# Three expert blocks of 512 tokens in place of six of 256, and one ring of four tiles for the first-layer results

## The chip, the core and the metric

The kernel runs on one core of one Trainium2 chip. The metric is the device time of one execution in microseconds (us), as the median of several runs. The engines are named as in the profile: PE is TensorE's matmul, PEld its weight load, DVE is VectorE, ACT ScalarE, POOL GpSimd, SP SyncE. A queue (SPq, POOLq) is where an engine issues transfers.

## The reference

An attention over 8 sequences of 576 tokens with 8 heads of 64 makes 4608 rows of 512 numbers; four heads see the last 32 positions, four see every 32nd. Its result goes through a mixture of 8 experts, of which each token uses one:

```python
logits = x @ w_gate + modality_bias[modality_id]
e_idx = np.argmax(logits, axis=1)
...
gate_w = probs[np.arange(N), e_idx]
for e in range(E):
    mask = e_idx == e
    h = np.maximum(x[mask] @ w1[e], 0.0)
    out[mask] = gate_w[mask, None] * (h @ w2[e])
```

`x` is 4608 x 512, `w1[e]` 512 x 1024, `w2[e]` 1024 x 512, all float32. With the inputs that the reference draws, three experts get all tokens. After the second pair of sequences they hold 731, 1115 and 458 tokens, after the third 1093, 1693 and 670, and at the end 1435, 2291 and 882 (worked out from the reference itself).

## The kernel before, in words

**Attention and routing.** 32 units (16 of local heads, 16 of strided) go through PE in an order written out by hand (L1250 to L1280). After each pair of sequences `finish_pair` turns rows and columns, and `route` computes the expert of each token, its place in the expert's region of a DRAM buffer `xd`, and nine scatters of 128 token rows each, which POOL issues (L687 to L699). The rows of a token are 528 words: 512 numbers, the token's number and its gate weight.

**Blocks.** The second half of the program is a row of expert blocks. A slot is 256 tokens of one expert (`SLOT`). `PHASES` says after which pair of sequences how many slots are drawn up: 2 after the second pair, 4 after the third, 20 places after the last. `slots` (L732) computes on DVE, with small instructions on tables of 8 experts, which expert and which rows each slot has; the first six slots are blocks of one slot each, the last phase has five blocks of two slots of one expert (`NDOUBLE`), two of one slot (`NSINGLE`), and one half slot of 128 tokens (`half_ffn`). Slots beyond those would run in a conditional part (`rest`, L1325), which is not taken here. The list of blocks is `plan` (L1190): six single blocks (names 0_0, 0_1, 1_0 to 1_3), five double ones, two single ones.

**One block, `ffn` (L1046).** Eight steps f, one for each 128 columns of the first layer. Step f brings the weights of f (1024 columns: 512 of each layer) into a high and a low part: ACT copies and rounds (`wh`, L1098), DVE subtracts (`wl`, L1101), two pieces of 512 each. `up` (L1050) is 12 matmuls into one PSUM bank, three products for each of the 4 pieces of 128: `wh`·`xh`, `wh`·`xl`, `wl`·`xh`; the stationary side is the weight, the moving side the tokens, so each streams 256 columns in a single block and 512 in a double one. ACT then makes `hh` (L1064), DVE the low part `hl` (L1065). `down` (L1068) is three matmuls of 512 columns for each 128 tokens: 6 in a single block, 12 in a double one. `down` of step f runs two steps later (`LAG`). In the last `down` ACT scales the sums by the gate weight (`y`, L1081) and POOL scatters them to the output (L1082).

**Buffers.** `hh` and `hl` of a single block come from two pools of four tiles; a double block takes four tiles `h2` in places that the attention used (`xc2`, `xc3`). `xh` and `xl` of single blocks have two buffers each of 256 columns, those of double blocks two of 512 (`xta`, `xtb`).

**Tokens of a block.** `gather` (L1211) has SP load the rows of a slot from `xd` (`fx`, L870), once all scatters up to that phase's pair of sequences have landed. `send` (L1218) copies the rows as 16-bit halves on DVE (`rows`, L1012, two instructions) and has SP transpose them, SBUF to SBUF (`cols`, L1018, two DMAs). `split` (L1222) copies them back on DVE (`xs`, L1029), ACT rounds the high part (`xh`, L1043), DVE subtracts the low part (`xl`, L1044). The first block takes another way: PE transposes its tokens (`turn_tokens`, L988, 8 transposes) and ACT and DVE split them. `between` (L1290) says at which step of block k what is done: gather of block k+3 in step 7, send of block k+2 in step 6 (its second slot in step 7), split of block k+1 in step 4 (second slot in step 5). It also takes up pieces of the routing of the last pair (`pop`).

**What sets the order.** In the attention PE's order is the one of the program; from the first block on a scheduler decides it when the program is built, on all engines. Each engine then works in that order. Blocks 0 and 1 still have PE work of the last pair's routing between their matmuls: 36 transposes of 128 x 128 (`xl`, `xs`), the gating matmuls (`lg`), three more transposes (`lt`) and a few small ones.

## Time and profile before

| | us |
|---|---|
| median of 3 runs | 574.73 (574.72 to 575.61) |
| the profiled execution | 579.18 |
| its span, first to last instruction | 577.1 |
| PE busy in it | 548.6 (95%) |
| DVE / ACT / POOL busy | 377.5 / 312.2 / 91.0 |
| DMA | 137.00 MB, mean 237 GB/s |

The profiled execution has its own time, 4.45 us over the median; 2.1 us of it lie outside the span. Durations below are of this execution. A row of the timeline has the start in us from the span's start, the length, engine, line, operation, what is written and read, shape and count; in square brackets stands how long the engine stood still before it and what ended that. Rows of equal instructions that overlap are merged. A matmul's length includes its way through the array, so the distance of two starts, not the length, is what a matmul costs.

### The profile page before, as it was taken

The page shows a single profiled execution, that of the slowest core. Times are in us where ns is not written, and L with a number is a line of the kernel's source. Part 1 is how long each engine was busy: PE and PEld are TensorE (multiplying, and loading weights), DVE is VectorE, ACT ScalarE, POOL GpSimd, SP SyncE. Part 2 cuts the span into 40 slices and gives each one's busy share as a digit, 9 for nine tenths or more (in the row PEclk, how much of TensorE's full clock was granted, in tenths as well). Part 3 has the DMA queues.
Part 4 walks back from the last instruction along what each step waited for, and adds up shares of the span by engine and source line. Part 5 has one row for each costly group of instructions (what it writes and reads, how often), then busy time and mean ns, then how long its engine had stood idle before and what let it go on. Part 6 is the DMA issues. An engine that isn't in the chain of part 4 may idle for free.

```text
span 577.1 us, 13498 instructions
## 1 busy us (share of the span) xinstructions
PE 548.6 (95%) x5273; PEld 462.5 (80%) x5273; DVE 377.5 (65%) x940; ACT 312.2 (54%) x651; POOL 91.0 (16%) x108
## 2 busy tenths in 40 slices
PE   7889789798999999999999999999999999999995
PEld 4777667676888999899988888888888888889984
DVE  7967867869967897787965735635734734547541
ACT  3657676658876566576653344344353443456642
POOL 2020230320612611011010020020020011021320
PEclk9979999999999999999999999999999999999998
DMA  7979888888989999999896582482482553455621
GB/s 262 349 232 316 290 279 285 291 316 276 411 220 344 408 318 411 286 332 277 270 258 259 154 268 78 136 284 92 118 249 109 148 179 114 126 199 176 247 92 39
DMA packets 65942, 137.00 MB, mean 237 GB/s; under 512 B 40383, under 2 KB 40767, under 8 KB 58816
## 3 DMA queue, kind: packets, MB, share of 16 engines
q1 hardware_dynamic: 59168, 112.46, 60.7%
q0 software_dynamic: 6416, 23.37, 11.0%
q8 instruction: 43, 0.70, 0.5%
q10 hardware_dynamic: 288, 0.24, 0.2%
q14 instruction: 27, 0.22, 0.1%
HBM read 107.97 MB, written 24.30 MB: 229 GB/s over the span
## 4 chain that ended last, share of the span: by engine, by line
PE 85%; DVE 5%; issue 4%; ACT 2%; DMA 2%; SPq 1%; POOL 0%; POOLq 0%; DVEq 0%; ACTq 0%
PE h L1056 35%; PE o L1074 35%; PE s L398 2%; PE o L446 2%; PE oa L544 2%; DMA lqk<-in_qkl 2%; PE xs L236 2%; PE ss L492 2%; PE lg L621 2%; PE xl L236 1%; PE t L236 1%; ACT xc L557 1%; PE ts L236 1%; DVE eb L530 1%; DVE mx L411 1%
## 5 line engine op out<-in xcount | busy, mean ns | idle before, releaser
L1056 PE MATMUL h<-xh,wh 128*128 128x256 f32 (+1 forms) x408 | 132.9, 326 | 0.2 <-ACT wh L1098 0.2
L1056 PE MATMUL h<-xh,wl 128*128 128x256 f32 (+1 forms) x408 | 132.8, 326 | 0.0
L1056 PE MATMUL h<-xl,wh 128*128 128x256 f32 (+1 forms) x408 | 132.6, 326 | 0.0
L1074 PE MATMUL o<-wh,h 128*128 128x512 f32 x320 | 105.8, 392 | 0.0
L1101 DVE TENSOR_TENSOR wl<-lqk,wh 128x512 fp32r<-128x512 f32 x104 | 68.0, 688 | 52.7 <-ACT wh L1098 46.6
L1098 ACT CAST wh<-raw 128x512 fp32r<-128x512 f32 x102 | 58.5, 622 | 58.7 <-PE o L1074 54.9
L1082 POOL DMA_INDIRECT out<-y,le x36 | 39.4, 1093 | 320.9 <-ACT y L1081 313.9
L1101 DVE TENSOR_TENSOR wl<-raw,wh 128x512 fp32r<-128x512 f32 x102 | 66.5, 689 | 32.5 <-ACT wh L1098 31.9
L1098 ACT CAST wh<-lqk 128x512 fp32r<-128x512 f32 x104 | 60.0, 620 | 49.7 <-PE o L1074 45.9
L1056 PEld LDWEIGHTS h<-xh,wh 128*128 128x128 f32 x408 | 77.3, 189 | 9.7 <-ACT wh L1098 0.4
L1056 PEld LDWEIGHTS h<-xl,wh 128*128 128x128 f32 x408 | 77.3, 189 | 8.9
L1056 PEld LDWEIGHTS h<-xh,wl 128*128 128x128 f32 x408 | 77.3, 189 | 7.7 <-DVE wl L1101 0.4
L1074 PEld LDWEIGHTS o<-wh,h 128*128 128x128 f32 x320 | 60.1, 188 | 13.7
L1074 PE MATMUL o<-wl,h 128*128 128x512 f32 x160 | 62.9, 393 | 0.0
L1065 DVE SCALAR_TENSOR_TENSOR h<-h,h 128x512 fp32r<-128x512 f32 x40 | 27.7, 692 | 48.9 <-ACT h L1064 48.9
L1064 ACT ACTIVATE h<-h 128x512 fp32r<-128x512 f32 x40 | 23.9, 599 | 50.3 <-PE h L1056 50.3
L1074 PE MATMUL o<-wh,hh 128*128 128x512 f32 x128 | 51.1, 399 | 0.0
L1074 PE MATMUL o<-wl,hh 128*128 128x512 f32 x128 | 50.5, 395 | 0.0
L1074 PE MATMUL o<-wh,hl 128*128 128x512 f32 x128 | 49.3, 393 | 0.0
L1064 ACT ACTIVATE hh<-h 128x256 fp32r<-128x256 f32 x64 | 24.6, 385 | 24.8 <-PE h L1056 22.7
L1074 PEld LDWEIGHTS o<-wl,h 128*128 128x128 f32 x160 | 30.0, 188 | 6.7
L689 POOL DMA_INDIRECT xd<-xa,posi x20 | 21.7, 1087 | 77.4 <-DVE eb L530 28.9
(211 smaller groups left out, 849.4 us busy)
## 6 DMA issues: line engine op xcount, KB each, us to landing
lqk<-in_w SPq DMA_DIRECT2D x26, 1024.0 KB
raw<-in_w SPq DMA_DIRECT2D x24, 1024.0 KB
lqk<-in_qkl SPq DMA_DIRECT2D x32, 296.0 KB
vv<-in_vl SPq DMA_DIRECT2D x32, 292.5 KB
sqk<-in_qks SPq DMA_DIRECT2D x32, 288.0 KB
fx<-xd SPq DMA_DIRECT2D x16, 528.0 KB
vs<-in_vs SPq DMA_DIRECT2D x16, 320.0 KB
xd<-in_nul SPq DMA_DIRECT2D x9, 528.0 KB
```

The source lines that it names most:

```text
L236: nc.tensor.transpose(dst, src, ident)
L398: nc.tensor.matmul(sp[32 * u:32 * u + 32, 128 * m:128 * m + 128], q[:, i, :], kd[:, :, i:i + 2, :], start=False, stop=True, skip_group_che ...
L446: nc.tensor.matmul(o[64 * jj:64 * jj + 64, k, :], et[:, 2 * (k // 2) + bb, 2 * (k % 2) + jj, :, :].rearrange("p g q -> p (g q)"), vv[:, 4 ...
L492: nc.tensor.matmul(s[32 * u:32 * u + 18, 36 * i:36 * i + 36], qk[:, 32 + r, :], qk[:, r:r + 65:64, :], start=False, stop=True, skip_group_ ...
L689: ins = nc.gpsimd.indirect_dma_start(xd[:], IOA(ap=posi[:, i:i + 1], axis=0), x[:, j, :], None)
L1056: nc.tensor.matmul(hp, wx[:, a1], x[:, c, :], start=(k == 0), stop=(k == 11))
L1064: evicted[f] = nc.scalar.activation(hh[:], hp, AF.Relu)
L1065: nc.vector.scalar_tensor_tensor(hl[:], hp, 0.0, hh.bitcast(F32), ALU.max, ALU.subtract)
L1074: nc.tensor.matmul(os[h], hx[:, m], w[:, 512:1024], start=(f == 0 and i == 0), stop=(f == 7 and i == 2))
L1082: outs.add(nc.gpsimd.indirect_dma_start(out, IOA(ap=le[:, 0:1], axis=0), y[:], None, bounds_check=NT - 1, oob_is_err=False))
L1098: ins = nc.scalar.copy(wh[:, c], raw[:, c])
L1101: nc.vector.tensor_tensor(wl[:, c], raw[:, c], wh[:, c].bitcast(F32), ALU.subtract)
```

## The change

`PHASES` now has 30 places in the last phase, and the first two phases are drawn up in pairs of slots: `slots` halves the number of full slots of each expert (`prs`) and gives out pairs. `plan` becomes three double blocks (0, 1_0, 1_1), then the five double, two single and the half block as before. The first block's 512 tokens are all turned by PE (`turn_first(0)`, `turn_first(1)`), its first `up` is made in two halves of 256 columns, and its step f now takes up routing pieces twice. All blocks share a ring of four tiles for `hh`/`hl`: two lie where the first weights `ws0`, `ws1` of the first block lay, two are new. `xh`/`xl` of 256 columns with two buffers become one of 512, used by block 0 and by the first of the two late single blocks. `cols` has one buffer. The table `PLACES` moves the token work: in a double block the next block's first slot is sent in step 2 and split in step 4, the second sent in step 4 and split in step 6, and the block after that gathered in step 5; in a single block the send is in step 1, the split and the gather in step 5.

```diff
-PHASES = ((1, 2), (2, 4), (3, 20))
+PHASES = ((1, 2), (2, 4), (3, 30))
-POPF = (2, 2)
+POPF = 2
-FIRST, SECOND, SPLIT, SEND, GATHER, FAR = 1, 3, 4, 6, 7, 6
-CPAD = 1216
+FIRST, SECOND = 1, 2
+PLACES = {2: (2, 4, 4, 6, 5), 1: (1, 5, 0, 0, 5)}
+CPAD = 1048
...
+        prs = smalls([P, E], I32, f"prs{ph}")
+        nc.vector.tensor_copy(prs[:], nblk[:])
+        nc.vector.tensor_single_scalar(prs[:], prs[:], 1, ALU.arith_shift_right)
+        sums(0, prs)
+        nc.vector.scalar_tensor_tensor(off[:, 0, :], exc[:, 0, :], -2.0, used[ph][:], ALU.mult, ALU.add)
...
+    def h_tile(f):
+        return ring[f % 4]
...
     def split_first(f):
-        w = ap.tile([P, 2, 512], F32R, tag=f"xc{2 + f}", bufs=2, name=f"ws{f}")
+        w = ap.tile([P, 2, 2 * SLOT], F32R, tag=f"xc{2 + f}", bufs=2, name=f"ws{f}")
+        ring.append(w)
...
+    def turned_pair(n):
+        return [pre.tile([P, 4, 2 * SLOT], F32R, tag=t, bufs=1, name=f"{t}{n}") for t in ("xh", "xl")]
...
-        if far:
-            cols = ap.tile([P, 2, 2, 4, P], U16, tag=f"xc{n[-1]}", bufs=1, name=f"cols{n}")
-        else:
-            cols = fp.tile([P, 2, 2, 4, P], U16, tag="cols", bufs=1, name=f"cols{n}")
+        cols = fp.tile([P, 2, 2, 4, P], U16, tag="cols", bufs=1, name=f"cols{n}")
...
         def up(f, wh, wl):
             hp = pa(f"h{n}{f}")[:, 0:w]
-            k = 0
-            for c in range(4):
-                a1 = slice(P * c, P * c + P)
-                for wx, x in ((wh, xh), (wh, xl), (wl, xh)):
-                    nc.tensor.matmul(hp, wx[:, a1], x[:, c, :], start=(k == 0), stop=(k == 11))
-                    k += 1
...
+            for q in (slice(0, SLOT), slice(SLOT, w)) if first and f == 0 else (slice(0, w),):
+                k = 0
+                for c in range(4):
+                    a1 = slice(P * c, P * c + P)
+                    for wx, x in ((wh, xh), (wh, xl), (wl, xh)):
+                        nc.tensor.matmul(hp[:, q], wx[:, a1], x[:, c, q], start=(k == 0), stop=(k == 11),
+                                         skip_group_check=first)
+                        k += 1
+            hh, hl = (h_tile(f + 2)[:, i, 0:w] for i in range(2))
...
-            slots_of = [(i,) for i in range(n)]
+            slots_of = [(2 * i, 2 * i + 1) for i in range(n // 2)]
...
         if n == nu + 1:
             while calm and next(calm[0], calm) is not calm:
                 pass
-            turn(0, split_first)
+            turn_first(0)
+    turn_first(1)
     scatter_rows(len(todo))
...
             if k == 0 and f == SECOND:
                 while 1 not in tables:
                     pop(1)
-                gather(2)
-            if f == SPLIT:
-                if k + 1 == len(plan):
-                    turn(k + 1)
-                split(k + 1, 0)
-            if f == SPLIT - 1 + parts(k + 1):
-                split(k + 1, 1)
-            if f == SEND:
-                send(k + 2, 0)
-            if f == GATHER:
-                gather(k + 3, 0)
-                send(k + 2, 1)
-                gather(k + 3, 1)
-            pop(POPF[k > 0])
+                load(1, 0)
+                gather(1, 0)
+                gather(1, 1)
...
+            for part in range(2):
+                if part < parts(k + 1):
+                    if f == sends[part]:
+                        send(k + 1, part)
+                    if f == splits[part]:
+                        split(k + 1, part)
+            if f == PLACES[parts(k)][4]:
+                gather(k + 2, 0)
+                gather(k + 2, 1)
+            pop(POPF)
```

Three places show how the built order moves. The names carry the block and the step: `h0_01` is block 0, step 1 after the change, `h0_01` before is block 0_0, step 1; the last number of a name is a counter. First PE at the start of the first block; `xt` are the tokens turned by PE, `oa` and `ob` the last unit of the attention. Before:

```order
L236 MATMUL xt0_00_3043<-cf_sb_65,fx0_00_2882 128x128 x4
L236 MATMUL xt0_01_3053<-cf_sb_65,fx0_00_2882 128x128 x4
L544 MATMUL oa15_3066<-eb15_3006,vs15_2880 64x126 x8
L551 MATMUL ob15_3075<-ec15_3007,vs15_2880 64x72 x2
L1056 MATMUL h0_00_3103<-xh0_0_3041,ws0_3050 128x256
```

With the change:

```order
L237 MATMUL xt000_3046<-cf_sb_65,fx00_2885 128x128 x4
L237 MATMUL xt001_3056<-cf_sb_65,fx00_2885 128x128 x4
L545 MATMUL oa15_3069<-eb15_3009,vs15_2883 64x126 x8
L552 MATMUL ob15_3078<-ec15_3010,vs15_2883 64x72 x2
L237 MATMUL xt010_3084<-cf_sb_65,fx01_2943 128x128 x4
L237 MATMUL xt011_3091<-cf_sb_65,fx01_2943 128x128 x4
L1057 MATMUL h0_00_3124<-xh0_3044,ws0_3053 128x256
```

Eight transposes stand ahead of the first matmul of the experts.

Second, ACT from the first token copy on (`xc33` is the attention's last result, `xc30` the routing's). Before:

```order
L984 CAST ws1_3060<-raw0_2836 128x512
L557 COPY xc33_143<-oa15_3066 128x28x18
L558 COPY xc33_143<-ob15_3075 128x4x18
L1098 CAST wh0_00_3095<-raw0_2836 128x512
L1098 CAST wh0_01_3099<-raw0_2836 128x512
L579 COPY xc30_140<-xl300_3195 128x512
L1064 ACTIVATE hh0_00_3116<-h0_00_3103 128x256
```

With the change:

```order
L985 CAST ws1_3063<-raw0_2839 128x512
L558 COPY xc33_143<-oa15_3069 128x28x18
L559 COPY xc33_143<-ob15_3078 128x4x18
L1095 CAST wh0_00_3116<-raw0_2839 128x512
L1095 CAST wh0_01_3120<-raw0_2839 128x512
L1003 CAST xh0_3044<-xt010_3084 128x2x256
L1003 CAST xh0_3044<-xt011_3091 128x2x256
L580 COPY xc30_140<-xl300_3215 128x512
```

The high part of the second 256 tokens stands behind two weight copies.

Third, DVE where the tokens of the first phase-1 slots are handled; `rows1_01` is the second slot of the next block, `wl0_06` the weights of step 6. Before, that slot's block is two blocks away:

```order
L1065 SCALAR_TENSOR_TENSOR hl0_06_3420<-h0_06_3406,hh0_06_3419 128x256
L1012 COPY rows1_00_3423<-fx1_00_3265 128x2x512 x2
L889 COPY le1_00_3429<-fx1_00_3265 128x8
L651 TENSOR_TENSOR lo3_3444<-lo3_3444,bias_68 128x8
L1101 TENSOR_TENSOR wl0_11_3537<-raw0_2836,wh0_11_3536 128x512 x2
```

With the change:

```order
L1062 SCALAR_TENSOR_TENSOR h0_3114<-h0_04_3423,h0_3114 128x512
L1030 COPY xs1_00_3438<-cols1_00_3268 128x1024 x2
L1098 TENSOR_TENSOR wl0_06_3471<-lqk1_84,wh0_06_3470 128x512 x2
L1044 TENSOR_TENSOR xl1_00_3442<-xs1_00_3438,xh1_00_3441 128x2x256
L685 TENSOR_TENSOR po3_3503<-rk3_3506,ohb3_3403 128x72
L1044 TENSOR_TENSOR xl1_00_3442<-xs1_00_3438,xh1_00_3441 128x2x256
L1016 COPY rows1_01_3447<-fx1_01_3260 128x2x512 x2
L887 COPY le1_01_3453<-fx1_01_3260 128x8
L1062 SCALAR_TENSOR_TENSOR h1_3115<-h0_05_3477,h1_3115 128x512
```

The copy back of the first slot (`xs1_00`), which waits for its transposes, now stands ahead of the weights of step 6 of the same block.

## Rows read from the trace of the kernel before

**Rows 1.** The page: tenths of PE busy and of its granted clock, 40 slices.

```profile
PE   7889789798999999999999999999999999999995
PEclk9979999999999999999999999999999999999998
```

**Rows 2.** Windows: stretch, length, busy PE PEld DVE ACT POOL, PE clock, DMA share, GB/s.

```profile
147.22:175.10 27.88, 27.71 (x216) 24.03 (x213) 21.52 (x60) 20.34 (x45) 11.40 (x9) 1.00 0.95 312
175.10:198.06 22.96, 22.96 (x150) 20.48 (x148) 20.43 (x53) 14.02 (x28) 11.28 (x11) 1.00 1.06 366
198.06:289.62 91.56, 91.56 (x584) 83.11 (x582) 74.88 (x177) 58.06 (x116) 10.07 (x9) 1.00 1.02 320
289.62:506.64 217.02, 217.02 (x944) 176.77 (x942) 114.40 (x186) 90.24 (x156) 19.21 (x18) 1.00 0.55 170
```

**Rows 3.** Timeline of PE: first matmul of successive steps in a single and two double blocks.

```profile
237.54 0.28 PE L1056 MATMUL h<-xh,wh 128*128 128x256 f32 x1
...
240.36 0.28 PE L1056 MATMUL h<-xh,wh 128*128 128x256 f32 x1
...
346.25 0.39 PE L1056 MATMUL h<-xh,wh 128*128 128x512 f32 x1
...
351.81 0.39 PE L1056 MATMUL h<-xh,wh 128*128 128x512 f32 x1
...
390.57 0.40 PE L1056 MATMUL h<-xh,wh 128*128 128x512 f32 x1
...
396.08 0.40 PE L1056 MATMUL h<-xh,wh 128*128 128x512 f32 x1
```

**Rows 4.** Timeline of PE: two neighbouring matmuls of 256 columns, and two of 512.

```profile
238.01 0.28 PE L1056 MATMUL h<-xl,wh 128*128 128x256 f32 x1
238.13 0.28 PE L1056 MATMUL h<-xh,wl 128*128 128x256 f32 x1
...
395.85 0.39 PE L1074 MATMUL o<-wh,h 128*128 128x512 f32 x1
```

**Rows 5.** Timeline of PE around the first matmul of the experts, and transposes further on.

```profile
145.06 1.09 PE L236 MATMUL xt<-cf_sb,fx 128*128 128x128 f32 x8
146.08 1.08 PE L544 MATMUL oa<-eb,vs 126*64 126x126 f32 x16
147.22 0.39 PE L1056 MATMUL h<-xh,ws 128*128 128x256 f32 x1
...
155.94 0.60 PE L236 MATMUL xl<-cf_sb,xa 128*128 128x128 f32 x4
156.37 0.60 PE L236 MATMUL xl<-cf_sb,xb 128*128 128x128 f32 x4
```

**Rows 6.** Groups of PE, 147.22 to 198.06: busy, mean ns | idle before, releaser.

```profile
L1056 PE MATMUL h<-xh,wh 128*128 128x256 f32 x57 | 16.3, 286 | 0.2 <-ACT wh L1098 0.2
...
L621 PE MATMUL lg<-xc,cz_sb 128*32 128x256 f32 x32 | 2.5, 385 | 0.0
```

**Rows 7.** Timeline of ACT at the start of the first block.

```profile
145.75 0.59 ACT L999 CAST xh<-xt 128x512 fp32r<-128x512 f32 x1
...
148.77 1.18 ACT L1098 CAST wh<-raw 128x512 fp32r<-128x512 f32 x2
```

**Rows 8.** Timeline of POOL and SP's queue and of DVE: the tokens of slot 1_0.

```profile
160.10 0.96 POOL L689 DMA_INDIRECT xd<-xb,posi  x1 [0.30 <-issue]
...
170.74 0.40 SPq L870 DMA_DIRECT2D fx<-xd  x1
...
174.47 1.29 DVE L1012 COPY rows<-fx 128x1024 uint16<-128x1024 uint16 x2 [1.54 <-DMA fx<-xd]
```

**Rows 9.** Timeline of SP's queue: pairs of token transposes.

```profile
197.10 7.28 SPq L1018 DMA_TRANSPOSE cols<-rows  x2
...
220.36 13.32 SPq L1018 DMA_TRANSPOSE cols<-rows  x2
...
297.06 2.63 SPq L1018 DMA_TRANSPOSE cols<-rows  x2
```

More of the change, by code (lines that the diff above doesn't have):

```diff
@@ L65 @@
 C_S2 = C_SIO + 32
-C_P = C_S2 + 20
+C_P = C_S2 + 30
 C_T = C_P + 1
@@ L785, in by_group @@
             return t.rearrange("p (g s) e -> p g s e", g=ng)
-        first = C_S2 if last else C_SIO
-        sio = cf[:, first:first + n].rearrange("p (g s) -> p g s", g=ng).unsqueeze(3).to_broadcast(sg)
+        sio = cf[:, C_S2:C_S2 + n].rearrange("p (g s) -> p g s", g=ng).unsqueeze(3).to_broadcast(sg)
         gi = smalls(sg, F32, f"gi{ph}")
@@ L1044, in split_tokens, with ffn @@
             nc.vector.tensor_tensor(xl[:, c, q], xs[:, c, :], xh[:, c, q].bitcast(F32), ALU.subtract)
-    def ffn(fp, n, xh, xl, les, between, load=None, first=False):
+    def ffn(fp, n, xh, xl, les, between, load=None, first=False, then=lambda f: None):
         os, evicted = [], {}
@@ L1108, in ffn @@
             wh, wl, up_w = ws.pop(f)
-            if load and f % 2:
+            if load and f % 2 and (f > 1 or not first):
                 load(f // 2)
@@ L1113, in ffn @@
             settle(LAG)
+            then(f)
     units, ends, complete, xts = [], {}, [False] * NBP, []
@@ L1219, in send @@
         if k < len(plan) and part < parts(k):
-            sent[k, part] = send_tokens(fp, f"{plan[k][0]}{part}", gathered[k, part], k >= FAR)
+            sent[k, part] = send_tokens(fp, f"{plan[k][0]}{part}", gathered[k, part])
     def split(k, part):
@@ L1224, in split, with turn_first @@
             split_tokens(fp, k, part)
-    def turn(k, *then):
-        if k == len(plan):
-            turned[k] = turn_half(gathered[k, 0])
-        if k < len(plan):
-            turned[k] = turn_tokens(plan[k][0], gathered[k, 0], *then)
+    def turn_first(part):
+        if not part:
+            turned[0] = *turned_pair("0"), []
+        xh, xl, les = turned[0]
+        les.append(turn_tokens("0", gathered[0, part], xh, xl, part, (lambda c2: None) if part else split_first))
     nu = len(units)
@@ L1288, in attention_moe @@
     empty(xd[0:SLOT, :])
+    ring += [fp.tile([P, 2, 2 * SLOT], F32R, bufs=1, name=f"h{i}") for i in range(2)]
     for k, (n, *_) in enumerate(plan):
+        sends, splits = PLACES[parts(k)][0:3:2], PLACES[parts(k)][1:4:2]
         def between(f):
             if k == 0 and f == FIRST:
-                send(1, 0)
                 over.append(True)
@@ L1296, in between @@
                     pop(1)
-                gather(2)
-            if f == SPLIT:
-                if k + 1 == len(plan):
-                    turn(k + 1)
-                split(k + 1, 0)
-            if f == SPLIT - 1 + parts(k + 1):
-                split(k + 1, 1)
-            if f == SEND:
-                send(k + 2, 0)
-            if f == GATHER:
-                gather(k + 3, 0)
-                send(k + 2, 1)
-                gather(k + 3, 1)
-            pop(POPF[k > 0])
+                load(1, 0)
+                gather(1, 0)
+                gather(1, 1)
+            if k + 1 == len(plan) and f == splits[0]:
+                turned[k + 1] = turn_half(gathered[k + 1, 0])
+            for part in range(2):
+                if part < parts(k + 1):
[7 more added lines that the diff above has]
+            pop(POPF)
             if blanks:
                 blanks.pop(0)()
-        ffn(fp, n, *turned[k], between, partial(load, k + 1), first=k == 0)
+        ffn(fp, n, *turned[k], between, partial(load, k + 1), first=k == 0,
+            then=lambda f: pop(POPF if parts(k) == 2 else 0))
     half_ffn(fp, *turned[len(plan)])
```

93 lines of the change are left out of this document (38 added, 55 removed).

## The prediction, made before the change was run

> **What bounds the kernel now.** I read the page's slices first. From the eleventh slice on (144 us) PE's digit is 9 in all slices but the last, and so is its clock's [rows 1]: the expert blocks run on a full PE at a granted clock of about 1.00, the 2.4 GHz level. Then the windows, cut at the first matmul of blocks. In the first block PE is busy 27.71 of 27.88 us, in the second 22.96 of 22.96, in the other four single blocks 91.56 of 91.56, in the four double blocks 217.02 of 217.02, at clock 1.00 each time; the second engine, DVE, has 21.52, 20.43, 74.88 and 114.40 [rows 2]. So a transfer or an engine other than PE counts only where it makes PE wait, and the question is how long PE takes for the same products in another shape. DMA is the other thing to see there: its share is 0.95 to 1.06 until 290 us, 0.55 in the double blocks. Third, the step distances: one single step costs PE 2.82 us, one double step 5.56 or 5.51 [rows 3]. The two values belong to the two `xh`/`xl` buffers, which alternate from block to block.
>
> **The sum**, against the profiled execution (579.18).
>
> 1. *The six single blocks' steps.* 48 single steps become 24 double ones. A pair of single steps is 2 x 2.82 = 5.64; one double step is 5.51 or 5.56. That is -0.13 or -0.08 for each of 8 steps of a block, -1.04 or -0.64 a block. Two neighbouring matmuls say the same from below: 0.12 at 256 columns, 0.23 at 512 [rows 4], so 24 x 0.12 - 12 x 0.23 = 0.12 saved for a pair. Block 1 should use the first buffer (-1.04), block 2 the second (-0.64). Block 0 has a buffer of its own; I take the middle, -0.84, and add 0.12 because its first `up` stays in two halves of 256: -0.72. Sum **-2.40**; bounds -1.8 and -3.0 (all blocks at the dearer or the cheaper value).
>
> 2. *Eight more transposes on PE.* Block 0's second 256 tokens are turned by PE ahead of the first expert matmul. Four transposes take 156.37 - 155.94 = 0.43 us, and eight 146.08 - 145.06 = 1.02 [rows 5], so 0.87 to 1.02. All of it is on the path, since PE does not stand still afterwards. I take **+0.95**.
>
> 3. *Waits of PE in block 0.* Before, from 147.22 to 198.06 PE does 16 `up` and 14 `down` of 256 tokens. An `up` of 12 matmuls at 0.12 is 1.44, a `down` the rest of 2.82, 1.38; 50.84 - 16 x 1.44 - 14 x 1.38 leaves 8.5 us. It is mostly the last pair's routing: 39 transposes at 0.108 are 4.2, the gating matmuls 2.5 [rows 6], small ones 0.2 or so. What remains, 1.5 us, bounds the waits that were there already; as idle time that the trace shows it is only 0.2, put down to ACT's `wh` [rows 6]. After the change the second half of step 0 needs `xh` of the second 256 tokens. Its transposes end near 148.1, and PE then has 12 x 0.12 = 1.4 us of the first half, to 149.6. ACT's order puts the two `wh` ahead of that cast; they ended at 149.95, a cast took 0.59 [rows 7], so `xh` is there at about 150.5: PE waits 0.9. A further 0.5 may be lost at step 2, whose `wh` is late behind `hh`. Waits so 1.4 against 1.5 before: **-0.1**, with bounds -1.5 (none) and +1.5 (ACT's four casts and the two halves of DVE's work in a row, all waited for).
>
> 4. *What I cost at nothing.* Weights are brought in and split once per 512 tokens: half of the loads, casts and subtractions of these blocks fall away, on engines and queues that PE does not wait for (DVE 74.88 of 91.56 [rows 2]); this only loosens the next term. Wider table work on DVE has 30 places instead of 20, and runs while PE has whole blocks ahead of it; with that cover gone I would put it under 0.3 us. Ring of four tiles: `hh` of step f is free again once `down` of step f has run, two steps later, as with two pools before; if it were tight, each step would show a stop, and the double blocks before, with four `h2`, show none. The late single blocks send their tokens in step 1 and split in step 5: three steps of 2.82 remain for copies and casts of about 5 us; no wait, up to 1 us if there is.
>
> 5. *The tokens of block 1.* This is the one new wait that could matter. Before, a slot was sent two blocks ahead; now it is sent in the block just ahead, and `cols` has one buffer. Block 1's first matmul should come at about 196: 198.06, less two `down` of 256 tokens that now lie behind it (2.8), less 0.7, plus 0.95, with up to a microsecond of doubt. On DVE the second slot is reached only after `xs1_00`, `wl0_06` and `xl1_00`, which follow step 4's `hl`. That one I put at 181: step 4's `up` ends after five `up` (13.9), 40 matmuls of `down` (9.2), nearly all routing (6.8) and the waits, counted from 148.2, near 179.5; then `hh` and `hl`. The copies in the row are at most 1.3 us each like the copy of `rows` [rows 8], so `rows1_01` is out by 186. Its transposes take 2.63 us in the quiet stretch, 7.28 or 13.32 in the crowded one [rows 9]; DMA carries half of the weights now, so I take 3 to 7: landed at 189 to 193. A copy of 1.3 and a cast of 0.6 make 191 to 195, just ahead of 196: **0**, and up to +7 with the slowest transposes.
>
> Sum: -2.40 + 0.95 - 0.1 = -1.55. The profiled execution becomes 577.6; it stands 4.45 us above the median, and I carry the difference over to the median: 574.73 - 1.55 = **573.2**. About 0.2% (1.15 us) is what a measurement of this kernel can tell from no change.
>
> **The rivals.**
>
> *No change, by the start.* Step 0 and 1 wait for everything that ACT and DVE do for 512 tokens in one chain, term 3's upper bound: -1.55 + 1.6 = +0.05 or a little less, 574.6. For it: ACT's order above, and ACT is busy 20.34 of the 27.88 us there [rows 2]. Against: PE has routing transposes to put between, as now.
>
> *Slower, by the tokens of block 1.* The gather of these rows was issued at 170.74, ten microseconds after POOL's last scatter at 160.10, and its first copy ran at 174.47 after a wait for the load [rows 8]. If that repeats, `rows1_00` is out at 175.8, and with transposes of 7.28 [rows 9] `xs1_00` starts not at 181 but at 183, holding up step 6's `wl` and then `rows1_01` until 188. 7.28 later, with 1.3 and 0.6, `xh` is complete at 197.2, 1.2 us late; with 13.32 it is 203.2, 7 late. I price it between, 4 us: -1.55 + 4 = +2.45, **577.2**. The point that decides is `rows1_01`: issued later than 187 it delays PE. For it: the DMA share is 1.06 just there [rows 2]. Against: the gather is now placed as early as step 2 of a block, and fewer weights are loaded.
>
> *No change, by the load.* The single steps were read where DMA was at 1.02, the double ones at 0.55 [rows 2, 3]. If their difference is not the shape but the load, a double step in the first 140 us costs as much as two single ones, the 2.40 falls away, and 0.95 - 0.1 = +0.85 remains: 575.6. Against: the distance of two neighbouring matmuls already shows it [rows 4], and it is the same in step after step. A rule of the Trainium skill points to it too: "TensorE: Matmul & The Clock Gate", section "Back-to-back issue gap", gives a single warm matmul N/2.4 + 2.5 ns for N columns, an estimate of 109 and 216 ns, by which 24 against 12 matmuls would save only 0.03 us a pair, 0.7 us in all. The trace disagrees with both figures (0.12 and 0.23), and its row decides.
>
> *The change does not do what it says.* If pairs left a slot over, the conditional blocks would run and cost tens of microseconds. The counts exclude it nearly: 731 and 1115 tokens of the first two experts after the second pair, 1693 and 670 after the third, are enough for full pairs, and the last phase has five doubles and two singles again.
>
> **How the numbers follow.** The forecast 0.55, its own range 571.9 to 574.3 (terms 1 and 2 at their bounds, half of term 3's). No change by the start 0.19, slower by the tokens 0.20, no change by the load 0.04, not what it says 0.02. The low end: -3.0 + 0.87 and term 3's lower bound is -3.6, 571.1; I take 571.3. The upper end leaves out the worse half of the slower rival: 576.8. Faster by over 0.2% means under 573.58: the forecast's larger part and a little of the rest, 0.48. Slower, above 575.88: the token rival and the last one, 0.22. Within: 0.30.
>
> **What would show it.** Right: double steps of about 5.5 us in the first three blocks, 16 token transposes of PE by the first expert matmul, a first matmul of block 1 near 196 and none of PE's stops above 1 us there. Start rival: idle time of PE before `h` released by ACT's `xh`, over 2 us. Token rival: idle time of PE at block 1 released by `xh` or `xl` of block 1, with DVE's `xs` waiting for the transposes. Load rival: steps of 5.64 in the first blocks. What makes the forecast wrong at once: steps over 5.6, or a stop of PE at each block's start.

## The result, and the profile after

With the change the kernel takes **569.79 us** (median of 6 runs, 567.96 to 571.82); the kernel before, measured beside it, 574.94 (6 runs, 574.42 to 575.83). The ratio is 0.9908, interval 0.9883 to 0.9933: faster by 5.2 us, where 573.2 was forecast, 1.5 less than the 574.73 shown. The time lies below the range given, 571.3 to 576.8. The profiled execution took 571.82, with a span of 570.0.

The page of the kernel after, busy tenths of PE and its granted clock, as in [rows 1]:

```profile
PE   6989799888999999999999999999999999999995
PEclk9989899999999999999999999999999999999999
```

PE is still the bound. Windows of the kernel after, cut at the first matmul of blocks 0, 1, 3 and 8 (the late singles), columns as in [rows 2]:

```profile
143.18:191.46 48.28, 47.53 (x273) 38.43 (x272) 32.79 (x91) 24.91 (x50) 13.76 (x13) 1.00 0.78 260
191.46:278.81 87.35, 87.35 (x380) 71.12 (x379) 52.46 (x120) 36.09 (x63) 13.05 (x13) 1.00 0.80 248
278.81:499.68 220.87, 220.87 (x960) 179.96 (x959) 113.21 (x183) 92.73 (x158) 21.42 (x20) 1.00 0.54 161
```

Blocks 1 and 2 are full, block 0 lost 0.75. (The windows don't compare one by one with [rows 2], because what hangs over into the next one, two `down`, is now of 512 tokens; they are compared at fixed places below.) DVE has 85.25 us of work in the first three blocks, where six had 116.83 [rows 2].

PE's timeline after, the start of the experts, to be read against [rows 5]:

```profile
139.94 1.33 PE L237 MATMUL xt<-cf_sb,fx 128*128 128x128 f32 x8
...
143.18 0.36 PE L1057 MATMUL h<-xh,ws 128*128 128x256 f32 x1
...
145.58 0.62 PE L1057 MATMUL h<-xh,ws 128*128 128x256 f32 x2 [0.72 <-ACT xh L1003]
```

Two things are to be seen. From the first token transpose (`xt`) to the first expert matmul it is now 3.24 us instead of 147.22 - 145.06 = 2.16, and PE waits 0.72 for the second half's `xh`: forecast. But the transpose itself comes 5.12 us earlier than in [rows 5]: not forecast, and not in the changed part. I therefore cut every profiled run at the first `xt`, and again at the first expert matmul `h`:

| us | first `xt` | first `h` | span | `xt` to end | `h` to end |
|---|---|---|---|---|---|
| before | 145.06 | 147.22 | 577.05 | 431.99 | 429.83 |
| after | 139.94 | 143.18 | 570.03 | 430.09 | 426.85 |

From `xt` to the end the change gained **1.90 us** in this pair of executions (forecast 1.55). The other 5.12 us between the two lie in the attention ahead of it. By 98.86 us of the kernel before 2.9 of them are there, and DVE's first different instruction comes only at 106.09.

PE's steps in blocks 1 and 2 of the kernel after, first matmul of successive steps, against [rows 3]:

```profile
195.58 0.39 PE L1057 MATMUL h<-xh,wh 128*128 128x512 f32 x1
...
201.08 0.40 PE L1057 MATMUL h<-xh,wh 128*128 128x512 f32 x1
...
239.67 0.39 PE L1057 MATMUL h<-xh,wh 128*128 128x512 f32 x1
...
245.23 0.39 PE L1057 MATMUL h<-xh,wh 128*128 128x512 f32 x1
```

That is 5.50 and 5.56. ACT's timeline after, the first `relu` of block 0 and the weights behind it:

```profile
149.99 0.60 ACT L1061 ACTIVATE h<-h 128x512 fp32r<-128x512 f32 x1 [2.00 <-PE h L1057]
150.49 1.14 ACT L1095 CAST wh<-raw 128x512 fp32r<-128x512 f32 x2
```

The `relu` follows PE's last matmul at once. In other runs this row looks different.

### The profile page after: what moved, and what is told of

Same layout as the page of the kernel before. It is cut to its first block, busy times and chain, and to the rows that moved or that the text cites. A ratio compares the mean times of both kernels' runs of the same rounds, so it can differ in the third digit from the quotient of the medians.

```text
span 570.0 us, 12704 instructions
## 1 busy us (share of the span) xinstructions
PE 542.6 (95%) x5005; PEld 447.6 (79%) x5005; DVE 346.7 (61%) x868; ACT 283.8 (50%) x579; POOL 89.4 (16%) x108
## 4 chain that ended last, share of the span: by engine, by line
PE 85%; DVE 4%; issue 4%; ACT 3%; DMA 2%; POOL 1%; SPq 1%; POOLq 0%; DVEq 0%; ACTq 0%
PE h L1057 35%; PE o L1071 35%; PE o L447 2%; PE s L399 2%; DMA lqk<-in_qkl 2%; PE lg L622 2%; PE xl L237 2%; PE oa L545 1%; PE xs L237 1%; PE ss L493 1%; PE t L237 1%; ACT xc L558 1%; PE ts L237 1%; DVE xa L462 1%; DVE mx L412 0%
## 5 line engine op out<-in xcount | busy, mean ns | idle before, releaser
L1057 PE MATMUL h<-xh,wh 128*128 128x512 f32 (+1 forms) x312 | 115.9, 371 | 0.0
L1057 PE MATMUL h<-xl,wh 128*128 128x512 f32 (+1 forms) x312 | 115.2, 369 | 0.0
L1057 PE MATMUL h<-xh,wl 128*128 128x512 f32 (+1 forms) x312 | 115.1, 369 | 0.0
L1071 PE MATMUL o<-wh,ws 128*128 128x512 f32 x288 | 96.8, 394 | 0.0
L1071 PEld LDWEIGHTS o<-wh,ws 128*128 128x128 f32 x288 | 54.1, 188 | 11.6
L1071 PE MATMUL o<-wl,ws 128*128 128x512 f32 x144 | 56.6, 393 | 0.0
L1062 DVE SCALAR_TENSOR_TENSOR ws<-h,ws 128x512 fp32r<-128x512 f32 (+1 forms) x40 | 25.5, 637 | 41.9 <-ACT ws L1061 41.8
L1061 ACT ACTIVATE h<-h 128x512 fp32r<-128x512 f32 (+1 forms) x40 | 22.2, 556 | 53.6 <-PE h L1057 53.6
L1062 DVE SCALAR_TENSOR_TENSOR h<-h,h 128x512 fp32r<-128x512 f32 (+1 forms) x40 | 25.4, 636 | 36.1 <-ACT h L1061 36.0
L1061 ACT ACTIVATE ws<-h 128x512 fp32r<-128x512 f32 (+1 forms) x40 | 22.2, 555 | 41.8 <-PE h L1057 41.8
L690 POOL DMA_INDIRECT xd<-xa,posi x20 | 21.7, 1084 | 101.3 <-ACT ws L1061 30.9
```

The source lines that it names most:

```text
L690: ins = nc.gpsimd.indirect_dma_start(xd[:], IOA(ap=posi[:, i:i + 1], axis=0), x[:, j, :], None)
L1057: nc.tensor.matmul(hp[:, q], wx[:, a1], x[:, c, q], start=(k == 0), stop=(k == 11), skip_group_check=first)
L1061: evicted[f] = nc.scalar.activation(hh, hp, AF.Relu)
L1062: nc.vector.scalar_tensor_tensor(hl, hp, 0.0, hh.bitcast(F32), ALU.max, ALU.subtract)
L1071: nc.tensor.matmul(os[h], hx[:, m], w[:, 512:1024], start=(f == 0 and i == 0), stop=(f == 7 and i == 2))
```

## The experiments

The kernels ran in five sittings, each on one chip, with runs of the kernel before beside them; a label's first letters name the sitting. Asked first: do the experts give more than the trace says, or does the attention ahead of them spread? And is it the width that makes the steps cheaper?

### First sitting: both again, the width alone, the loads in the old order

`c1_before_again` and `c1_after_again` have no edit. `c1_narrow` does each `up` of blocks 0 to 2 in two halves of 256:

```diff
-for q in (slice(0, SLOT), slice(SLOT, w)) if first and f == 0 else (slice(0, w),):
+for q in (slice(0, SLOT), slice(SLOT, w)) if narrow or first and f == 0 else (slice(0, w),):
...
+ narrow=k < 3)
```

`c1_early_old` issues the first loads of weights and tokens in the order of the kernel before:

```diff
-        for part in range(2):
-            paced(expert_weights(0, 0, 0, part))
...
+        for j in range(2):
+            for part in range(2):
+                paced(expert_weights(0, 0, j, part))
...
+        for h in range(2):
+            paced(half(1, h))
```

> The kernel before, unchanged, to see how much of the gap between the two profiles is chance. Between the two profiles PE reaches the first expert matmul 4.0 us earlier after the change, 0.8 of extra transposes included, so the attention ahead of it is 4.9 us shorter, and already 2.9 shorter at a place up to which both programs are the same. Theory 1 (chance in the attention): this profile has its first token transposes anywhere from 140 to 145 us, and the spread of the runs covers some 3 us. Theory 2 (the attention is really shorter after the change, by its other early loads and tables): first token transposes at 143 to 145 us again, time 574.4 to 575.8. From the first expert matmul to the end 429.8 us within 0.5 by both.

> The changed kernel, unchanged. From the first expert matmul to the end 426.9 us within 0.5. Theory 1 (chance): the first token transposes come between 139 and 145 us, no earlier on the mean than in the kernel before. Theory 2 (the attention is really shorter): at 139 to 141 us again. Ratio to before 0.988 to 0.994.

> The changed kernel with every first-layer step of the first three blocks made in two halves of 256 columns; pairs, loads and weight splits stay as changed. It undoes only the wider matmul. If the gain of the blocks is the wider matmul: steps of 5.62 to 5.64 in place of 5.51 and 5.56, 23 steps, together +2.1 us to +2.4 us against the changed kernel, 571.9 to 572.2. If it is the halved weight traffic or work off PE: no more than 0.3 us slower.

> The changed kernel with the early loads of the first block in the order of the kernel before (weights 0 and 1, first 256 tokens in between, weights 2, second 256 tokens, weights 3); everything else as changed. If the other order of these loads shortens the attention by about 2 us, this run is 1.5 to 2.5 us slower than the changed kernel, with the first token transposes that much later. If not: within 0.5 us, or slower only by a wait for the second 256 tokens at the first expert step, which the profile would name.

In this table and those below, the ratio and its interval are the ones on record; they are not the quotient of the two medians, from which the ratio differs by up to 0.005.

| run | median | ratio to before (577.05), interval | first `xt` | `xt` to end |
|---|---|---|---|---|
| c1_before_again | 578.50 | 1.0020 (0.9990 to 1.0051) | 142.75 | 434.45 |
| c1_after_again | 580.51 | 1.0034 (0.9996 to 1.0072) | 144.03 | 436.77 |
| c1_narrow | 582.84 | 1.0098 (1.0060 to 1.0137) | 142.85 | 437.82 |
| c1_early_old | 583.04 | 1.0097 (1.0064 to 1.0130) | 141.15 | 440.73 |

The gain did not come back. The first `xt` comes later in the change than in the kernel before this time (144.03 and 142.75), as in the second and the fourth sitting: nothing shows that coming earlier belongs to the change. And a loss lies behind the first `xt`: 436.77 where the first run had 430.09. It is one stop in block 0. ACT, then PE of `c1_after_again` there, then windows ahead of the stop, in it and behind it (columns as in [rows 2]):

```profile
158.41 0.60 ACT L1061 ACTIVATE h<-h 128x512 fp32r<-128x512 f32 x1 [6.54 <-issue]
158.90 1.13 ACT L1095 CAST wh<-raw 128x512 fp32r<-128x512 f32 x2
...
154.58 0.40 PE L1057 MATMUL h<-xh,ws 128*128 128x512 f32 x1
159.56 0.79 PE L1057 MATMUL h<-xh,wh 128*128 128x512 f32 x1 [4.59 <-ACT wh L1095]
```

```profile
150.00:155.00 5.00, 4.98 (x33) 4.16 (x32) 3.78 (x24) 1.24 (x3) 3.78 (x4) 1.00 1.01 408
155.00:159.50 4.50, 0.00 (x0) 0.00 (x0) 0.46 (x1) 1.09 (x3) 1.99 (x3) 0.80 0.82 315
159.50:164.50 5.00, 4.94 (x16) 4.15 (x17) 3.49 (x9) 3.22 (x7) 0.00 (x0) 0.50 0.21 48
164.50:169.50 5.00, 5.00 (x26) 4.17 (x25) 0.29 (x1) 0.92 (x2) 0.00 (x0) 1.00 0.94 366
```

PE has done the `up` of two steps by 155 and stops. ACT is idle and yet starts the first `relu` only at 158.41; behind it stand the weights `wh` of step 2, and behind those PE. When PE resumes, the granted clock is at 0.50, the 1.2 GHz level, for five microseconds. The stop and the clock make block 0 55.16 us long instead of 48.28. Nothing that the profile shows released that `relu` ("issue").

`c1_narrow` has the same stop (6.12 us), so its total says nothing on width. Its steps do, in blocks 1 and 2: 5.56 and 5.55, where 5.62 to 5.64 was expected and the wide ones take 5.51 and 5.56. PE there, the first matmul of successive steps in both blocks, then two matmuls of 256 columns in an `up` and two of 512 in a `down`:

```profile
217.13 0.28 PE L1057 MATMUL h<-xh,wh 128*128 128x256 f32 x1
...
222.69 0.28 PE L1057 MATMUL h<-xh,wh 128*128 128x256 f32 x1
...
261.57 0.28 PE L1057 MATMUL h<-xh,wh 128*128 128x256 f32 x1
...
267.12 0.28 PE L1057 MATMUL h<-xh,wh 128*128 128x256 f32 x1
...
206.72 0.28 PE L1057 MATMUL h<-xh,wh 128*128 128x256 f32 x1
206.84 0.28 PE L1057 MATMUL h<-xl,wh 128*128 128x256 f32 x1
...
208.85 0.40 PE L1071 MATMUL o<-wh,ws 128*128 128x512 f32 x1
209.08 0.39 PE L1071 MATMUL o<-wl,ws 128*128 128x512 f32 x1
```

By whole steps the width of `up` is worth 0.05 us in block 1 and nothing in block 2. The mean distances of neighbouring starts show two things in that. In `up` they are 117.9 ns against 229.0 (block 1) and 233.6 (block 2) in the kernel after, so 24 narrow matmuls against 12 wide ones cost 0.08 and 0.03 us more. But `down`, whose instructions the edit left alone, came closer as well, from 230 or 231 ns to 227. Why it did is open.

`c1_early_old` pays for the load order besides. PE:

```profile
147.54 2.33 PE L237 MATMUL xt<-cf_sb,fx 128*128 128x128 f32 x8 [4.15 <-DMA fx<-xd]
```

The second 256 tokens come 4.15 us too late for their transposes: the new order of loads is a needed part of the change.

### Second sitting: what the late `relu` holds up

`c2_before_third` and `c2_after_third` have no edit. `c2_follow_xh` puts ACT's `wh` of step 2 behind the second half's `xh` cast instead of behind the first `relu`; `c2_whole_first` does the first `up` in one piece:

```diff
-                    follow(ins, evicted[f - 2])
+                    follow(ins, evicted[f - 2] if f > 2 else turned_last[3])
```

```diff
-            for q in (slice(0, SLOT), slice(SLOT, w)) if first and f == 0 else (slice(0, w),):
+            for q in (slice(0, w),):
```

> The kernel before once more. Both theories: from the first expert matmul to the end 429.8 to 432.3 us; no relu of block 0 later than 1 us after its matmuls other than by work of ACT. What it shows besides: when the first token transposes come (142.8 and 145.1 us in the two profiles so far; 139.9 and 144.0 in those of the changed kernel). If they spread over the same 4 us in both kernels, the attention's share of the first result is chance.

> The changed kernel once more. In the first run of it block 0 took 48.3 us, in the second 55.2: PE waited 4.6 us for wh of step 2, which stood on ACT behind the first relu, and that relu started 4.6 us after its matmuls' end; the clock then fell to 0.50 for 6.8 us. Theory A (a stop that belongs to the change and comes in most executions, the first run being the lucky one): relu late by over 2 us again, block 0 55 us, total 3 to 8 us above the first run. Theory B (it belongs to the chip or to that call): block 0 at 48.3 us, ratio to before 0.988 to 0.994.

> The changed kernel, but ACT rounds the weights of step 2 right behind the second xh, ahead of the copies of the routing and of the first relu, no longer behind that relu. Theory A (PE stops because wh of step 2 waits behind a late relu): PE's stop before step 2 goes or shrinks to under 2 us and the clock stays at 1.00, so 4 to 7 us faster than the changed kernel on the same chip where the relu is late; where the relu is in time, within 0.7 us of it. If PE stops as long as before, at the first down of step 0 now, the late relu itself holds it and the order on ACT is not the price.

> The changed kernel with the first expert step in one piece of 512 columns, not in two halves. By my sum: the two halves cost 0.12 us of matmul time and hide 1.4 us of the wait for the second xh, so without them 0.9 to 1.3 us slower. If the late relu of the second run comes from the two halves in one PSUM bank, it is in time here, and this kernel 5 to 7 us faster than the changed one on the same chip.

| run | median | ratio to before (577.88), interval | first `xt` | `xt` to end |
|---|---|---|---|---|
| c2_before_third | 576.87 | 0.9978 (0.9941 to 1.0015) | 141.42 | 431.99 |
| c2_after_third | 579.94 | 1.0024 (0.9985 to 1.0063) | 143.40 | 436.53 |
| c2_follow_xh | 575.12 | 0.9968 (0.9924 to 1.0012) | 140.31 | 432.82 |
| c2_whole_first (4 runs) | 574.32 | 0.9891 (0.9814 to 0.9967) | 142.07 | 432.98 |

The late `relu` again. The trace's semaphore events show what it waited for: in `c2_after_third` the `up` of steps 0 and 1 ended at 153.18 and 154.34, and their semaphores landed together, at 158.36 and 158.43. PE of `c2_follow_xh`, then of `c2_whole_first`:

```profile
156.05 0.50 PE L1071 MATMUL o<-wh,h 128*128 128x512 f32 x1 [1.15 <-ACT h L1061]
```

```profile
147.42 0.73 PE L1057 MATMUL h<-xh,ws 128*128 128x512 f32 x2 [2.09 <-ACT xh L1003]
```

In the first the `relu` was as late (its semaphore landed at 155.38, its `up` was done at 150.55), but with no weights behind it PE stops 1.15 us instead of the 5.20 of `c2_after_third` (another 1.43 follow at 169.72, behind DVE): it is the queue behind the `relu` that costs. In the second the first `relu` came in time and the second 1.5 us late, and PE pays 2.09 at the start instead; behind that stop the granted clock is at 0.50 from 148.1 to 151.5 us.

### Third sitting: POOL's scatters, and the place of the tokens

`c3_after_fourth` has no edit. `c3_scatter_late` holds back POOL's last five scatters until the first `relu` is done, by a small copy that reads its result; `c3_whole_best` joins the two edits of the second sitting; `c3_block2_pre` gives block 2 the token buffer of block 0:

```diff
-    scatter_rows(len(todo))
+    scatter_rows(len(todo) - 5)
...
+            if k == 0 and f == 0:
+                t = cp.tile([P, 1], F32, name="gate")
+                nc.gpsimd.tensor_copy(t[:], ring[2][:, 0, 0:1].bitcast(F32))
+                scatter_rows(len(todo))
```

```diff
-            if k == len(plan) - NSINGLE:
+            if k in (2, len(plan) - NSINGLE):
```

> The changed kernel, as the reference on this chip. Late relu in block 0 (over 2 us after its matmuls) and block 0 near 55 us, as in two of three profiles; total 578 to 582. If this is a chip like that of the first result: relu in time, block 0 48.3 us, 568 to 572.

> The changed kernel, but POOL issues the last five of the nine scatters of the third pair only after the first relu. In the four late runs that relu started 1.8 to 2.5 us after POOL issued its last scatter of an unbroken row at 1.27 us each, and PE's semaphores arrived in one bunch then. Theory P (the row of scatters on POOL holds PE's semaphores back): relu 0 within 0.5 us of its matmuls, no stop of PE over 1 us before step 2, block 0 near 48.5 us; 4 to 7 us faster than the changed kernel where that one is late, less up to 4 us if the later gather delays block 1. Theory Q (something else holds the relu): relu late by 2 us or more though POOL issues nothing at that time.

> The changed kernel with the first step in one piece and with ACT's order changed: both xh of the second 256 tokens right after their transposes, then the weight copies of steps 0 to 2, all ahead of the first relu. Against one piece alone (574.3 with a wait of 2.1 us for xh): the wait shrinks to about 1.0 us and wh of step 2 no longer waits behind a late relu. Expected 571 to 574 us and faster than the kernel before by 0.5 to 1 percent. If a late relu holds PE at the first down anyway, 574 to 577.

> The changed kernel, but the tokens of block 2 lie in the buffer of block 0 (where the single blocks had theirs before), not in one of the pair that takes turns. The run with halves of 256 columns had 5.56 and 5.54 us a step in blocks 1 and 2, no more than whole steps of 512 (5.51 and 5.56), while two single steps of the kernel before took 5.64. Theory W (width): block 2 at 5.51 to 5.56 as with the other buffers. Theory L (the place of the tokens in SBUF): block 2 at 5.62 to 5.64 a step, 0.6 us more in the block.

| run | median | ratio to before (573.56), interval | first `xt` | `xt` to end |
|---|---|---|---|---|
| c3_after_fourth | 570.60 | 0.9939 (0.9906 to 0.9972) | 138.41 | 430.34 |
| c3_scatter_late | 570.67 | 0.9960 (0.9937 to 0.9983) | 136.32 | 430.49 |
| c3_whole_best | 570.59 | 0.9939 (0.9917 to 0.9961) | 141.51 | 430.13 |
| c3_block2_pre | 573.27 | one run | 140.71 | 430.77 |

Here the unchanged kernel had its `relu` in time (148.78), and 430.34 repeats the first run's 430.09; so the late scatters had nothing to mend, and `c3_whole_best` gave back at the start what it saved. For the place, PE in block 2 of `c3_block2_pre`, successive steps:

```profile
240.90 0.39 PE L1057 MATMUL h<-xh,wh 128*128 128x512 f32 x1
...
246.34 0.39 PE L1057 MATMUL h<-xh,wh 128*128 128x512 f32 x1
```

5.44 a step, where the second ring buffer has 5.56 and the first 5.51, for the same instructions. Neither theory had a step below 5.5: the price of a step depends on where its tokens lie. It is not only the moving operand's own place: `up` went from 233.6 to 226.7 ns a matmul, but `down`, which moves weights, also went from 230.7 to 226.7. In this same buffer single steps take 2.82 (the first late single block of the kernel after):

```profile
508.04 0.28 PE L1057 MATMUL h<-xh,wh 128*128 128x256 f32 x1
...
510.86 0.28 PE L1057 MATMUL h<-xh,wh 128*128 128x256 f32 x1
```

Two of them are 5.64, so there one wide step saves 0.20 us, where `c1_narrow` gave 0.05 or nothing.

### Fourth sitting: with and without the scatters

`c4_before_fourth` and `c4_after_fifth` have no edit, `c4_scatter_late` is the kernel of the third sitting. `c4_best2` is `c3_whole_best` with the buffer of block 0 for every even block (`if k % 2 == 0`).

> The kernel before, in one call with the changed one. From the first expert matmul to the end 429.8 us (up to 432.3 with a wait for the routing). Theory 1 (the attention's share of the first result is chance): first token transposes within 3 us of those of the changed kernel, in either order, and the medians of the two differ by -2 to -3.5 us where no relu is late. Theory 2 (the attention is really shorter after the change): transposes 4 to 5 us later than in the changed kernel, medians 5 us apart.

> The changed kernel. From the first expert matmul to the end 426.8 us with the first relu in time, 433.5 with it late; total 568 to 572 or 578 to 582. Theory 1 and 2 as for the kernel before.

> The last five scatters of the third pair after the first relu, again. If the changed kernel has its relu late in this call: theory P (POOL's row of scatters holds PE's semaphores) has it in time here, 426.8 us from the first expert matmul to the end; theory Q has it late here too. If the changed kernel has it in time, both are at 426.8 and the question stays open.

> One piece in the first step and ACT's other order as before, and besides the tokens of every even block in the buffer of block 0. Block 2 there had 5.44 us a step in place of 5.56. If that place is cheap for every block: blocks 2, 4, 6 at 5.44, the odd ones taking turns at 5.51 and 5.56, together -2.1 us against the changed kernel; 568 to 570 where no relu is late, and 1 percent faster than the kernel before. If it was chance of that run: steps of 5.51 and 5.56 again.

| run | median | ratio to before (577.27), interval | first `xt` | `xt` to end |
|---|---|---|---|---|
| c4_before_fourth | 576.66 | 1.0004 (0.9967 to 1.0042) | 140.63 | 432.70 |
| c4_after_fifth | 580.25 | 1.0048 (1.0020 to 1.0076) | 143.46 | 435.71 |
| c4_scatter_late | 572.71 | 0.9933 (0.9893 to 0.9973) | 139.79 | 430.47 |
| c4_best2 | 573.67 | 0.9908 (0.9873 to 0.9944) | 143.33 | 429.52 |

ACT and PE of `c4_after_fifth`, with POOL's last scatter, and one window behind the stop:

```profile
157.05 0.60 ACT L1061 ACTIVATE h<-h 128x512 fp32r<-128x512 f32 x1 [5.77 <-remote]
...
158.21 0.50 PE L1057 MATMUL h<-xh,wh 128*128 128x512 f32 x1 [3.80 <-issue]
...
156.05 0.96 POOL L690 DMA_INDIRECT xd<-xb,posi  x1 [0.30 <-issue]
```

```profile
159.50:162.50 3.00, 3.00 (x10) 2.42 (x9) 2.13 (x5) 1.67 (x4) 0.00 (x0) 0.51 0.18 32
```

The `relu` starts 1.0 us after the last scatter of the row (1.8 in `c1_after_again`, 2.4 in `c2_after_third`). ACT and POOL of `c4_scatter_late`, on the same chip:

```profile
149.61 0.60 ACT L1061 ACTIVATE h<-h 128x512 fp32r<-128x512 f32 x1 [2.00 <-PE h L1057]
...
146.05 0.96 POOL L690 DMA_INDIRECT xd<-xa,posi  x1 [0.30 <-issue]
150.28 0.19 POOL L1292 COPY gate<-h 128x1 f32<-128x1 f32 x1 [3.26 <-ACT h L1061]
154.54 0.98 POOL L690 DMA_INDIRECT xd<-xa,posi  x1 [4.08 <-DMA xd<-in_nul]
```

The `relu` is in time, block 0 takes 48.29, the clock stays at 1.00, and from `xt` to the end the kernel gains 435.71 - 430.47 = 5.24 us. All ten runs of `c4_after_fifth` took longer (578.28 to 582.36) than any of `c4_scatter_late` (570.35 to 578.07). So moving the five scatters takes the delay away, in a sitting in which it is there. Whether POOL's instructions hold the semaphores or the transfers that they start is not told apart. The row is not enough by itself: in the first run and in the third sitting it ran over the same place (to 153 and 152) and the `relu` was in time. Nor do the semaphores always wait for its end. ACT and POOL of `c4_best2`, whose first `up` was done at 153.36:

```profile
155.55 0.60 ACT L1061 ACTIVATE h<-h 128x512 fp32r<-128x512 f32 x1 [4.21 <-PE h L1057]
...
155.94 0.96 POOL L690 DMA_INDIRECT xd<-xb,posi  x1 [0.30 <-issue]
```

There the `relu` is 2.2 us late and still starts ahead of the last scatter. With the weights ahead of it on ACT, PE has no stop above 1.1 us, and blocks 2, 4 and 6 run at 5.44 a step. What a sitting with late semaphores adds stays open.

### Fifth sitting: towards a better version

`c5_late_even` joins the late scatters and the even blocks' buffer; `c5_late_even_order` adds the `follow` edit of the second sitting with the `xh` casts ahead of all three `wh`.

> The changed kernel with the last five scatters after the first relu and the tokens of every even block in the buffer of block 0. From the first token transpose to the end 430.5 us with late scatters alone; the places take 2.1 us off (blocks 2, 4, 6 at 5.44 a step; blocks 1 and 5 at 5.51, 3 and 7 at 5.56): 428.4. Median 0.9 to 1.2 percent under the kernel before, whether or not the changed kernel would have its relu late in this call.

> The same, and ACT rounds xh of the second 256 tokens ahead of the weights of steps 0 to 2. PE's wait of 0.7 us for that xh goes, so 0.3 to 0.7 us less from the first token transpose to the end, 427.7 to 428.1; if the weight copies are then late for the first down, nothing gained.

| run | median | ratio to before (573.85), interval | first `xt` | `xt` to end |
|---|---|---|---|---|
| c5_late_even | 568.51 | 0.9933 (0.9900 to 0.9966) | 137.26 | 428.70 |
| c5_late_even_order | 570.46 | 0.9924 (0.9890 to 0.9959) | 140.69 | 429.12 |

The even blocks run at 5.44 a step, and `c5_late_even` has the shortest way from `xt` to the end, 1.4 us under the change and 3.3 under the kernel before (428.4 was expected). Its ratio is 0.7% under the kernel before, 0.3 to 1.0, where 0.9 to 1.2 was expected. The last edit takes PE's wait for the second `xh` away and gets another one, at block 1:

```profile
192.74 0.50 PE L1057 MATMUL h<-xh,wh 128*128 128x512 f32 x1 [1.83 <-ACT xh L1043]
```

That is the rival "tokens of block 1" in small: a block 0 that is done earlier stands before tokens that are not there. By the way from `xt` to the end `c5_late_even` is the version to keep; the ratios don't tell the two apart, and neither was timed beside the change itself in one sitting.

## Why the prediction was right and wrong

**The sum held, from the first `xt` on, in the pair shown**: -1.90 measured, -1.55 forecast. That it is so close is partly luck. The four profiled executions of the kernel before took 431.99 to 434.45 us from `xt` to the end (the longest has a wait of 1.62 us for the last pair's routing), the two of the change with its first `relu` in time 430.09 and 430.34; so pairs of them give a gain of 1.7 to 4.4. A second cut, at the fifth step of the first block behind the changed ones, tells the terms apart; PE before, then after:

```profile
307.54 0.40 PE L1056 MATMUL h<-xh,wh 128*128 128x512 f32 x1
```

```profile
300.61 0.40 PE L1057 MATMUL h<-xh,wh 128*128 128x512 f32 x1
```

From the first `h` that is 160.32 before and 157.43 after, -2.89; behind it, to the end, 269.51 and 269.42.

- *Term 1.* Blocks 1 and 2 have 5.51 and 5.56 a step, as put, so -1.68 as forecast. Block 0 with its waits is the rest, 2.89 - 1.68 = 1.2 us shorter, where terms 1 and 3 together gave 0.82. The cause was put half right: by `c1_narrow` and `c3_block2_pre` the gain against 2 x 2.82 is that of the place together with the width, not of the width alone. With halves of 256 columns the two blocks already had 5.56 and 5.55, so only 0.05 of the 0.13 a step in block 1, and none of the 0.08 in block 2, went with the width. The load rival is out: block 1 ran its steps of 5.51 at a DMA share of 0.94 (195.58 to 228.61 us), and in the kernel before single steps took 2.82 at 1.02 [rows 2] and at 0.62 (515 to 534 us) alike.
- *Term 2.* `xt` to `h` grew by 1.08 for the eight transposes; forecast 0.95.
- *Term 3.* The wait for `xh` was put at 0.9 and is 0.72, where it was put; 0.5 more at step 2 did not come.
- *Term 4.* No stop at the ring of four, none in the late singles.
- *Term 5.* No stop of PE at block 1's first matmul, 48.28 after the first `h`. The forecast had it at 196, counted from 148.2: 47.8.
- *Two slips that move nothing.* The window of 217.02 us [rows 2] holds five double blocks, not four. By the rule given for the forecast's own range its upper end is 574.7, not 574.3.

**The step that failed is the last one of the sum: "it stands 4.45 us above the median, and I carry the difference over to the median".** That takes the first 145 us as equal. They are not equal in one and the same kernel: the first `xt` came between 140.6 and 145.1 in four executions of the kernel before, and between 138.4 and 144.0 in five of the change, in the first run earlier after the change and in the fourth sitting later. The waits view of PE, before (to 145 us) and after (to 140.1; engine, line, releaser: total, times, longest), shows the same two places with other lengths; below them, the windows up to the first `xt`, before and after, columns as in [rows 2]:

```profile
PE o L446 <- issue: 5.7, 3, 2.8
PE ss L492 <- issue: 3.3, 7, 0.9
```

```profile
PE o L447 <- issue: 4.3, 2, 2.3
PE ss L493 <- issue: 2.6, 2, 1.5
```

```profile
0.00:145.06 145.06, 123.35 (x2957) 98.83 (x2958) 110.57 (x400) 91.00 (x231) 24.86 (x49) 0.98 0.85 290
0.00:139.94 139.94, 120.08 (x2958) 98.05 (x2958) 110.42 (x402) 90.84 (x231) 25.13 (x49) 0.98 0.86 299
```

The waits are the smaller part. PE was idle 21.7 us before and 19.9 after, 1.8 of the 5.12; the rest is time that counts as busy, for as many matmuls at the same granted clock. Where it arises stays open.

The range had no term for the spread of these 145 us. By this pair of executions 1.9 of the 5.2 us are the change's. That the remaining 3.3 are the attention's spread fits the two executions, but is not shown for the medians of that sitting, since one execution of each kernel was profiled; with the kernel before at 434.45 in place of 431.99, up to 4.4 would be the change's.

**And a rival was missing, on the slower side**: ACT's first `relu` waiting for PE's semaphores behind POOL's scatters, with two steps' worth of queue behind it. In three of the five profiled executions of the change it made the way from `xt` to the end 3.7 to 4.8 us longer than the 431.99 of the kernel before. My start rival named the right place (the chain `xh`, `relu`, `wh` on ACT) but priced it by what ACT has to do, 1.6 us. It was the arrival of an event that made it long, and the clock's lower level that made it dearer. With it goes the result: the same change came out at 0.9908 and 0.9939 where the profiled `relu` was in time, and at 1.0034, 1.0024 and 1.0048 where it was late.

**Open.** Why the semaphores come late in some sittings: one and the same chip had it in the first and not in the third. The kernel before was slower too in those three sittings (577.05 to 577.88, against 573.56 to 574.94). Many of the trace's own event records are missing in the same stretch (in `c1_after_again` no landing is recorded that could have released the first `relu`), so a share of the recording in the delay isn't excluded. Block 0's second tokens turned by DMA instead of PE, and ACT without any given order, weren't tried.

## What to carry to other kernels

Cut a profile at the first instruction that the change touches, and give each side of the cut its own spread: a sum that comes out to 0.4 us in one pair of executions says little of a total whose untouched part moves by five. Where an engine's queue holds the next steps' operands behind an event of another engine, price the event's arrival too, not only the work. Before a gain is put down to an instruction's width, run that width from another buffer.

## What the runs showed of the hardware

- In `c2_after_third` PE's semaphores for two finished steps landed 5.2 and 4.1 us after their matmuls, and together, in a stretch with an unbroken row of POOL's indirect scatters, one each 1.27 us; in `c4_scatter_late`, with five scatters moved, ACT started 0.04 us after PE's last matmul, as in the first run.
- Around stops of PE of 2.09 us (`c2_whole_first`) to 6.12 us (`c1_narrow`) in block 0 the granted clock fell to 0.50, the lower of its two levels, and stayed there for 3.4 to 6.8 us.
- Two neighbouring matmuls of 512 columns were on the mean 227 to 234 ns apart, by the buffer of the block's tokens, and whole steps took 5.44, 5.51 or 5.56 us. By the Trainium skill, "TensorE: Matmul & The Clock Gate", section "Back-to-back issue gap", a single warm matmul of 512 columns takes an estimate of 216 ns and a sustained stream 131. No buffer here reaches either, and the measurement decides.
